# Backward pass of a conditioned spectral and gated block on one core: three loads in the tail are issued at other places

## The chip, the cores and the metric

The kernel runs on one core of a Trainium2 chip. The core has TensorE (PE, matrix products; its weight loads are listed as PEld), VectorE (DVE), ScalarE (ACT), GpSimd (POOL) and SyncE (SP). Each engine works through its own instruction queue in order; semaphores order work between them. DMA transfers are issued here by SP and by POOL and are carried by the core's 16 DMA engines. The metric is the device time of one execution in microseconds (us); a lower time is better. A kernel is timed in several runs, and the median is given.

## The reference

The reference returns the output of a block and the gradients of all its inputs but one. The forward pass, with x of 2048 rows by 576 columns in bfloat16, is

```python
mod = (silu(c) @ w_mod)                 # six rows of 576: sa, ca, ga, sb, cb, gb
h = layernorm(x) * (1 + ca) + sa
x = x + ga * irfft2(rfft2(h) * (w_r + 1j * w_i))      # spectral filter
h = layernorm(x) * (1 + cb) + sb
x = x + gb * (((h @ w_gate) * (h @ w_up)) @ w_down)   # 4608 hidden columns
```

and the kernel computes this output (out_0), the gradients of A_x (out_1), of w_r and w_i (out_2, out_3), w_gate, w_up and w_down (out_4 to out_6), c (out_7) and w_mod (out_8), for a given gradient of the output.

## The kernel before

The 2048 rows lie in 16 tiles of 128 rows, the hidden columns in 36 blocks of 128. The program has three large parts. The first (from line 217) makes the modulation rows, the spectral filter forward, and the gradient of the hidden product (ghhT). The second, which fills most of the time, walks over the 36 hidden blocks: gate and up products (line 647), the gradient with respect to the normalised rows, accumulated by DVE (lines 676 and 681), and the three weight gradients (u57p, line 594). The third part, the tail (from line 731), is where the change lies. It has four stages that overlap:

- the *norm stage* (t1_norm, t1_turn, t1_cols, t1_rows): for each row tile, the backward of the second layernorm, then the forward transforms of the gradient into the buffer Vp. Every second tile, SP loads n2c, goc and yc (two row tiles each, two buffers; line 857). The products n2c with ghr (csA, line 791) and yc with gxr (csC) are column sums for the modulation gradients. The last six weight-gradient products (u57p of the last two hidden blocks) are dealt out between the tiles as filling for PE, and their results are turned and stored by SP (woT, lines 605 to 607).
- the *filter stage* (t2_turn to t2_grad): 19 groups of up to 16 frequencies. Per group four transpositions (trv), products with BD2 (xp), the multiplication with the filter by DVE (fm, line 198, reads wn), transpositions back (try_) and products with BDA (apt). Every fourth group also makes its filter gradient (filter_grad), which loads Xn by POOL and writes its result over wn.
- the *inverse stage* (t3_rows, t3_cols, t3_norm): per row tile the inverse transforms with the tables GB (upa, upb) and IR (yp), and the backward of the first layernorm, with loads n1c and gxc and the store of out_1.
- the *down projection* (u3p, line 1127): out_0 needs for each of 16 row tiles and two halves 36 matmuls of hl (loaded back from hhT_d, nine hidden blocks at a time) with w_down, which lies in wdA (15 blocks) and wdB (21 blocks). These 1152 matmuls depend on none of the three stages; they fill PE's gaps in them and then run alone. The filter gradients that are left (rest) and the modulation sections run beside them.

What sets the order: the kernel is written in a tile framework whose scheduler lays down one fixed order per engine when the program is built, from data dependencies, priorities and a model of costs. The norm stage has raised priority (line 921). `tc.issue_after(ins)` puts what it holds behind `ins` on the engine of `ins`; it adds no wait for the transfer's end. `load_table(pool, key, tag, engine)` loads a constant table into a named slot: RD and IR share slot tA, G1 and GB share tB. Each DMA queue has eight semaphore slots, so an issue waits for the transfer eight places ahead of it.

The places that the change touches: the tile zero (line 757), which is the operand that opens and closes column-sum banks; wn's load from its copy in memory, wn_d, by POOL (line 939); the loads of GB and IR by POOL (lines 1011 and 1012); and wdA's load, in two parts, behind the yc load of tiles 4 and 5 (lines 1100 to 1105).

Of the kernel before, what the change touches and what calls it, by code (L numbers as in the profile page):

```python
# [10 lines left out]
BF = mybir.dt.bfloat16  # L11
# [8 lines left out]
NT = 16  # L20
# [4 lines left out]
FP = 292  # L25
# [59 lines left out]
def build(ctx, tc, A_x, A_w_r, A_w_i, B_w_gate, B_w_up, B_w_down, c_in, w_mod, grad_out,  # L85
          out_0, out_1, out_2, out_3, out_4, out_5, out_6, out_7, out_8):
    nc = tc.nc
# [130 lines left out]
    with ExitStack() as hs:  # L218
        def pool(name, bufs, side="left", space=None, stack=hs):
            kw = dict(name=name, bufs=bufs, reuse_waits="tile")  # L220
            if space is not None:
                kw["space"] = space
            else:
                kw["side"] = side
            return stack.enter_context(tc.tile_pool(**kw))
# [505 lines left out]
    with ExitStack() as ts:  # L731
# [9 lines left out]
        ps_cs = pool("ps_cs", 1, space=PSUM)  # L741
        ps_u3 = pool("ps_u3", 2, space=PSUM)
        tl0 = pool("tl0", 1)
        o2p = pool("o2p", 2)
        oAp = pool("oAp", 1)
        oBp = pool("oBp", 1)
        tl = pool("tl", 1)
        Vp = pool("vp", 1).tile([128, NG, 128], BF, name="b_Vp")
        tl3 = pool("tl3", 1)

        def modh(j, name, pool, eng=nc.sync):
            m = pool.tile([128, D], BF, name=name)
# [1 line left out]
            return m  # L754

        T = {}
        zero = tl3.tile([128, 512], BF, name="zero")
        nc.gpsimd.memset(zero[:], 0.0)
        Vv = Vp[:].rearrange("k g (t c f) -> k g t c f", t=NT, c=2)
        gb_h = modh(MGB, "gb_h", tl, nc.gpsimd)  # L760
# [79 lines left out]
        with ExitStack() as r1:  # L840
            c1 = pool("c1", 2, "right", stack=r1)
            c1b = pool("c1b", 1, "right", stack=r1)
            csA = ps_cs.tile([128, 512], FP32, name="csA")
            csB = ps_cs.tile([128, 512], FP32, name="csB")
            csC = ps_cs.tile([128, 512], FP32, name="csC")
            rings = {k: c1b.tile([128, 3, DP], BF, name=k) for k in ("gyr", "ghr", "gxr")}
            with tc.high_priority(HEAD_START):
                for k in rings:
                    nc.vector.memset(rings[k][:, :, D:DP], 0.0)
            ld, gyTs, zts = {"order": []}, {}, {}  # L850

            def t1_norm(t):
                if t % 2 == 0:
                    for k, src in (("n2c", n2_d), ("goc", go_v), ("yc", y_d)):
                        ld[k] = c1.tile([128, 2, D], BF, name=k)
                        with behind(ld["order"]):
                            ins = nc.sync.dma_start(ld[k][:], src[:, t:t + 2, :])
                        if t == 4:
                            ld["after"] = ins.ins
                    if t < 4:  # L860
                        ld["order"] = [ins.ins]
                        with behind(ld["order"]):
                            for k, tag in ((("RD", "tA"),), (("G1", "tB"), ("BD2", None), ("BDA", None)))[t // 2]:
                                T[k] = load_table(tl0, k, tag)
                        ld["order"] = [tab_ins[k]]
                    ld[t // 2] = (ld["n2c"], ld["yc"])
                n2 = ld["n2c"][:, t % 2, :]
                gh, gx, gy = (rings[k][:, t % 3, 0:D] for k in ("ghr", "gxr", "gyr"))
                nc.scalar.copy(gh, acc(t))
                s12 = c1.tile([128, 2], FP32, name="s12")  # L870
                gn = c1.tile([128, D], BF, name="gn2")
                nc.vector.scalar_tensor_tensor(out=gn[:], in0=acc(t), scalar=1.0, in1=opcb_h[:], op0=MUL, op1=MUL, accum_out=s12[:, 0:1])
                jk = c1.tile([128, D], BF, name="jk2", bufs=1)
                nc.vector.scalar_tensor_tensor(out=jk[:], in0=gn[:], scalar=1.0, in1=n2, op0=MUL, op1=MUL, accum_out=s12[:, 1:2])
                ab = c1.tile([128, 2], FP32, name="ab2")
                nc.vector.tensor_scalar(out=ab[:], in0=s12[:], scalar1=-1.0 / D, scalar2=rstd2g[:, t:t + 1], op0=MUL, op1=MUL)
                u = c1.tile([128, D], BF, name="u2")
                nc.scalar.activation(out=u[:], in_=gn[:], func=ACT.Identity, bias=ab[:, 0:1], scale=rstd2g[:, t:t + 1])
                v = c1.tile([128, D], BF, name="v2", bufs=1)
                nc.vector.scalar_tensor_tensor(out=v[:], in0=n2, scalar=ab[:, 1:2], in1=u[:], op0=MUL, op1=ADD)  # L880
                nc.vector.tensor_tensor(out=gx, in0=v[:], in1=ld["goc"][:, t % 2, :], op=ADD)
                nc.gpsimd.dma_start(gx1_d[:, t, :], gx)
                nc.vector.tensor_tensor(out=gy, in0=gx, in1=ga_h[:], op=MUL)

            def t1_turn(t):
                pt = ps_fp.tile([128, 5, 128], BF, name="trp", tag="fp")
                for m in range(5):
                    nc.tensor.transpose(pt[:, m, :], rings["gyr"][:, t % 3, wide(m)], ident[:])
                gyTs[t] = c1.tile([128, 5, 128], BF, name="gyT")
                nc.scalar.copy(gyTs[t][:], pt[:])  # L890
                gh, gx = rings["ghr"][:, t % 3, :], rings["gxr"][:, t % 3, :]
                n2c, yc = ld[t // 2]
                if t == 0:
                    add_zero(csA, csB, csC, first=True)
                for h in range(2):
                    colsum(csB, h, gh[:, h * 288:(h + 1) * 288])
                diag(csA, csB, 288, gh, n2c[:, t % 2, :])
                diag(csC, csB, 352, gx, yc[:, t % 2, :])
                if t == NT - 1:
                    add_zero(csA, csB, csC, first=False)  # L900

            def t1_cols(t):
                zt = zts[t] = c1.tile([128, 2, FP], BF, name="zt")
                for cc in range(2):
                    zp = ps_fp.tile([128, 512], FP32, name="zp", tag="fp")
                    for m in range(5):
                        with behind(fill[t - 1:t] if t else []):
                            nc.tensor.matmul(zp[:, :FP], lhsT=gyTs[t][:, m, :], rhs=T["RD"][:, m, cc, :], start=(m == 0), stop=(m == 4))  # L908
                    nc.scalar.copy(zt[:, cc, :], zp[:, :FP])

            def t1_rows(t):
                zt = zts[t]
                for cc in range(2):
                    vp = ps_fp.tile([128, 512], FP32, name="vp", tag="fp")
                    nc.tensor.matmul(vp[:, :FP], lhsT=T["G1"][:, t, 0, :], rhs=zt[:, cc, :], start=True, stop=False)
                    nc.tensor.matmul(vp[:, :FP], lhsT=T["G1"][:, t, 2 if cc == 0 else 1, :], rhs=zt[:, 1 - cc, :], start=False, stop=True)
                    evac(Vv[:, :, t, cc, :], vp[:, :FP].rearrange("k (g f) -> k g f", f=4), eng=("a" if cc == 0 else "v"))

            steps = [t1_norm, t1_turn, t1_cols, t1_rows]
            for k in range(NT + len(steps) - 1):  # L920
                with tc.high_priority(HEAD_START + SPREAD * k):
                    for s_ in reversed(range(len(steps))):
                        if 0 <= k - s_ < NT:
                            steps[s_](k - s_)
            after = ld["after"]
            dcb = diag_rows(tl, csA, csB, 288, "dcb")
            dga = diag_rows(tl, csC, csB, 352, "dga")
            dsb = tl.tile([128, 288], FP32, name="dsb")
            nc.vector.tensor_copy(dsb[:], csB[:, 0:288])
# [6 lines left out]
        rA = ts  # L936
        ra = pool("ra", 1, "right", stack=rA)
        wn = ra.tile([128, 2, NT, FP], BF, name="wn2")
        nc.gpsimd.dma_start(wn[:].rearrange("k c a f -> k (c a f)"), wn_d)
        fg = pool("fg", 2, "right", stack=rA)  # L940
        rB = ExitStack()
        A_ = planes(pool("rb", 1, "right", stack=rB), "j_A")
        gYs = {}

        def dims(ci):
            ng = min(4, NG - 4 * ci)
# [2 lines left out]
        def filter_grad(ci):  # L949
            g0, ng, f0, w = dims(ci)  # L950
            Xn = fg.tile([128, 2, NT, 16], BF, name="Xn2")
            nc.gpsimd.dma_start(Xn[:].rearrange("k c a f -> k (c a f)"), xn_d[:, ci * 512:(ci + 1) * 512])
            t1 = fg.tile([128, 2, 2, NT, 16], FP32, name="gwt", bufs=1)
            for i in range(2):
                if w == 16:
# [7 lines left out]
        with ExitStack() as r2:  # L963
# [44 lines left out]
                    filter_grad(ci)  # L1008

            pipeline(NCH, [t2_turn, t2_filter, t2_back, t2_inv, t2_grad])  # L1010
        T["GB"] = load_table(tl0, "GB", "tB", nc.gpsimd)
        T["IR"] = load_table(tl0, "IR", "tA", nc.gpsimd)
        r3 = ExitStack()
        c3 = pool("c3", 2, "right", stack=r3)
        c3b = pool("c3b", 1, "right", stack=r3)
# [81 lines left out]
        wdA = oAp.tile([128, 15, D], BF, name="wdA")  # L1097
        wdB = oBp.tile([128, NFB - 15, D], BF, name="wdB")

        def wd_load(dst, k, f0, n):  # L1100
            with tc.issue_after(after):
                nc.sync.dma_start(dst[:, k:k + n, :], B_w_down[f0 * 128:(f0 + n) * 128, :].rearrange("(j f) d -> f j d", f=128))

        wd_load(wdA, 0, 0, 8)
        wd_load(wdA, 8, 8, 7)
        prs = {}
        for tp_ in range(NT // 2):
            hls = []
# [118 lines left out]
```

## Time and profile before

| | |
|---|---|
| runs | 1585.85, 1587.19, 1590.39 us; median 1587.19 |
| profiled execution: span from first to last instruction (its own time is listed in no other form) | 1583.9 us, 29938 instructions |
| PE busy | 1526.4 us, 96% |
| DVE busy | 1043.3 us, 66% |
| ACT busy | 559.4 us, 35% |
| POOL busy | 172.3 us, 11% |
| mean granted clock of TensorE | 0.990 |
| DMA | 280.33 MB, 177 GB/s on average |
| tail, 1230 to 1584 us: PE busy | 316.6 us |

The page gives busy time and idle time by engine, the waits by what ended them, the chain of work that ended last, and the DMA issues with their time from issue to landing. A busy PE is not a PE at its peak, because matmuls are pipelined and their ends are modelled: a u3p matmul of 288 columns is listed with 0.286 us, but 72 of them follow each other in 8.82 us. Idle time of an engine that is not the bound costs nothing. Positions are microseconds from the start of the span.

### The profile page before, as it was taken

The numbers are of one execution on the slowest core, as the hardware profiler recorded it, in microseconds if no ns is written. First come the engines' busy times: TensorE is split into PE (matmuls) and PEld (weight loads), VectorE is DVE, ScalarE is ACT, GpSimd is POOL, SyncE is SP. The second block draws the span as 40 slices with busy tenths as digits, with TensorE's granted clock in tenths as the row PEclk, the third lists the DMA queues.
The fourth block names the chain that finished last, engine by engine and source line by source line (L and its number), as shares of the span: only waits on it lengthen the run. The fifth ranks groups of instructions, "written<-read, shape, count | busy, mean of one in ns | idle before, by whom it ended". The sixth has DMA issues, their size and how long they took to land.

```text
span 1583.9 us, 29938 instructions
## 1 busy us (share of the span) xinstructions
PE 1526.4 (96%) x11300; PEld 1028.1 (65%) x11306; DVE 1043.3 (66%) x2626; ACT 559.4 (35%) x1120; POOL 172.3 (11%) x285
## 2 busy tenths in 40 slices
PE   6999999999999999999999999999999979799997
PEld 4665543566666666667666666766666666577775
DVE  6866663766666666666666666666666765678655
ACT  6667732322222222222222222222222356465022
POOL 0001221110010101001010100101000002000232
PEclk9999999999999999999999999999999999999999
DMA  9879997868685795877767786858976777547775
GB/s 323 268 197 235 289 261 211 172 133 158 123 177 114 159 153 118 168 132 155 141 148 136 143 163 122 173 116 144 139 141 137 193 207 200 212 144 214 278 228 156
DMA packets 485252, 280.33 MB, mean 177 GB/s; under 512 B 407634, under 2 KB 452435, under 8 KB 484211
## 3 DMA queue, kind: packets, MB, share of 16 engines
q1 hardware_dynamic: 459922, 185.50, 54.9%
q0 software_dynamic: 25184, 92.92, 19.7%
q8 instruction: 88, 1.44, 0.4%
q14 instruction: 58, 0.47, 0.1%
HBM read 108.48 MB, written 82.31 MB: 120 GB/s over the span
## 4 chain that ended last, share of the span: by engine, by line
PE 81%; DVE 6%; DMA 5%; issue 4%; ACT 3%; POOL 0%; SPq 0%; ACTq 0%; DVEq 0%; POOLq 0%
PE u57p L594 26%; PE u8p L676 18%; PE gup L647 16%; PE u4p L408 7%; PE u3p L1127 4%; PE gup L642 2%; DMA Xn<-xn_d 2%; DMA n2c<-n_d 2%; PE yp L186 1%; PE zp L908 1%; ACT u L1055 1%; PE zp L346 1%; DVE ln_st L151 1%; DMA xc<-in_A_x_dram 1%; DMA hh_sf<-hhT 1%
## 5 line engine op out<-in xcount | busy, mean ns | idle before, releaser
L681 DVE TENSOR_TENSOR acc<-acc,u8p 128x288 f32<-128x288 f32 x1088 | 489.2, 454 | 314.6 <-PE u8p L676 314.2
L676 PE MATMUL u8p<-wT,ggT 128*128 128x288 bf16 x1152 | 327.5, 286 | 1.7 <-DVE acc L681 1.7
L676 PE MATMUL u8p<-wT,guT 128*128 128x288 bf16 x1152 | 327.2, 286 | 0.0
L647 PE MATMUL gup<-h2T,wgu 128*128 128x512 bf16 x1152 | 294.9, 379 | 0.0
L597 ACT CAST so<-u57p 128x288 bf16<-128x288 f32 x216 | 86.0, 398 | 521.4 <-PE u57p L594 515.5
L594 PE MATMUL u57p<-gon,hh_sf 128*128 128x288 bf16 x1152 | 188.5, 286 | 0.5 <-DMA hh_sf<-hhT 0.5
L594 PE MATMUL u57p<-h2p,gg_sf 128*128 128x288 bf16 x1152 | 187.9, 286 | 0.0
L594 PE MATMUL u57p<-h2p,gu_sf 128*128 128x288 bf16 x1152 | 185.9, 286 | 0.0
L647 PEld LDWEIGHTS <-wgu 128*128 128x128 bf16 x1152 | 109.5, 98 | 98.8 <-issue 17.1
L676 PEld LDWEIGHTS <-ggT 128*128 128x128 bf16 x1152 | 112.6, 98 | 67.2 <-issue 14.0
L408 PE MATMUL u4p<-goT,wdT 128*128 128x512 bf16 x656 | 151.6, 380 | 0.6 <-DVE goT L380 0.5
L676 PEld LDWEIGHTS <-guT 128*128 128x128 bf16 x1152 | 112.7, 98 | 55.8 <-issue 2.2
L1127 PEld LDWEIGHTS <-hl 128*128 128x128 bf16 x1152 | 111.9, 99 | 32.9 <-issue 5.9
L594 PEld LDWEIGHTS <-hh_sf 128*128 128x128 bf16 x1152 | 112.7, 98 | 29.2 <-DMA hh_sf<-hhT 0.8
L594 PEld LDWEIGHTS <-gu_sf 128*128 128x128 bf16 x1152 | 112.5, 98 | 28.4
L594 PEld LDWEIGHTS <-gg_sf 128*128 128x128 bf16 x1152 | 112.5, 98 | 28.2
L649 ACT CAST gT<-gup 128x512 bf16<-128x512 f32 x144 | 84.3, 586 | 130.7 <-PE gup L647 130.7
L649 ACT CAST uT<-gup 128x512 bf16<-128x512 f32 x144 | 84.3, 585 | 73.5 <-PE gup L647 73.5
L408 PEld LDWEIGHTS <-wdT 128*128 128x128 bf16 x656 | 61.4, 98 | 73.1 <-issue 8.0
L1127 PE MATMUL u3p<-wdB,hl 128*128 128x288 bf16 x672 | 94.8, 290 | 5.3 <-DMA wdB<-in_B_w_down_dram 5.3
L660 POOL DMA_DIRECT2D hhT_d<-hhT x36 | 33.2, 921 | 504.4 <-DVE hhT L651 475.5
L141 ACT CAST ghh_st<-u4p 128x512 bf16<-128x512 f32 x88 | 51.2, 585 | 65.2 <-PE u4p L408 63.7
(357 smaller groups left out, 1701.7 us busy)
## 6 DMA issues: line engine op xcount, KB each, us to landing
ghhT_d<-ghh_st POOLq DMA_DIRECT2D x36, 512.0 KB, 4.4
ghh<-ghhT_d POOLq DMA_DIRECT2D x36, 512.0 KB, 7.3
hhT_d<-hhT POOLq DMA_DIRECT2D x36, 512.0 KB, 6.6
hl<-hhT_d SPq DMA_DIRECT2D x32, 576.0 KB, 7.2
out_dram<-woT SPq DMA_DIRECT2D x72, 128.0 KB, 2.0
wdn<-in_B_w_down_dram SPq DMA_DIRECT2D x18, 288.0 KB, 3.9
out_dram<-so SPq DMA_DIRECT2D x36, 144.0 KB, 2.6
wgu<-in_B_w_gate_dram SPq DMA_DIRECT2D x18, 256.0 KB, 3.4
```

What stands on the lines that cost most here:

```text
L141: nc.scalar.copy(dst, src)
L151: nc.vector.bn_stats(out=st[:, t, h, :], in_=xt[:, t, h * 288:(h + 1) * 288])
L408: nc.tensor.matmul(pt[:], lhsT=wdTs[k][:, j, m, :], rhs=goT[:, 4 * sb4:4 * sb4 + 4, m, :], start=(m == 0 and n == 5), stop=(m == n - 1))
L594: mm = nc.tensor.matmul(pw[0][:, 0:288], lhsT=sf[:, t, :], rhs=rhs_n[:, t, h * 288:(h + 1) * 288], start=(t == 0), stop=(t == NT - 1))
L597: nc.scalar.copy(so[:, h * 288:(h + 1) * 288], pw[0][:, 0:288])
L642: nc.tensor.matmul(pts[-1][:], lhsT=wgu[r, 8, jw * 128:(jw + 1) * 128], rhs=h2T[r, 4 * sb4:4 * sb4 + 4, 4, :], start=True, stop=False)
L647: nc.tensor.matmul(pts[k][:], lhsT=wgu[:, 4 * wi_ + m, jw * 128:(jw + 1) * 128], rhs=h2T[:, ts_, m, :], start=False, stop=(m == 3))
L649: nc.scalar.copy((gT, uT)[wi_][:, ts_, :], pts[k][:])
L660: nc.gpsimd.dma_start(hhT_d[:, :, fb, :].rearrange("tp f x -> f tp x"), hhT[:].rearrange("f (tp ti) p -> f tp (ti p)", ti=2))
L676: nc.tensor.matmul(pu[:, 0:288], lhsT=l_, rhs=r_, start=(k == 0), stop=(k == len(mms) - 1))
L681: nc.vector.tensor_tensor(out=dst, in0=dst, in1=pu[:, 0:288], op=ADD)
L1127: mm = nc.tensor.matmul(p2[:, 0:288], lhsT=hls[fb // 9][:, fb % 9, ti * 128:(ti + 1) * 128], rhs=(wdA[:, fb] if fb < 15 else wdB[:, fb - 1 ...
```

## The change

Four places of the tail are edited.

- The filter copy wn is loaded by SP instead of POOL, in two halves, behind the last of the norm stage's loads (`ld["final"]`, yc of tiles 14 and 15).
- wdA is loaded in three parts of five blocks instead of two parts of eight and seven; the parts are put behind the yc loads of tiles 6, 8 and 10 (`ld["y", t]`) instead of 4.
- The loads of GB and IR, still on POOL, are put behind the Xn loads of the groups 4 and 8.
- The tile zero moves from a pool of its own at the end into the pool of the tables, so that what lies between them in memory moves up by its 1 KB per partition.

```diff
         tl0 = pool("tl0", 1)
+        zero = tl0.tile([128, 512], BF, name="zero")
         o2p = pool("o2p", 2)
...
-        tl3 = pool("tl3", 1)
...
-        zero = tl3.tile([128, 512], BF, name="zero")
         nc.gpsimd.memset(zero[:], 0.0)
...
                             ins = nc.sync.dma_start(ld[k][:], src[:, t:t + 2, :])
                         if t == 4:
                             ld["after"] = ins.ins
+                        ld["final"] = ld["y", t] = ins.ins
...
-        nc.gpsimd.dma_start(wn[:].rearrange("k c a f -> k (c a f)"), wn_d)
+        for c in range(2):
+            with tc.issue_after(ld["final"]):
+                nc.sync.dma_start(wn[:, c].rearrange("k a f -> k (a f)"), wn_d[:, c * NT * FP:(c + 1) * NT * FP])
...
-        gYs = {}
+        gYs, xn_in = {}, {}
...
-            nc.gpsimd.dma_start(Xn[:].rearrange("k c a f -> k (c a f)"), xn_d[:, ci * 512:(ci + 1) * 512])
+            xn_in[ci] = nc.gpsimd.dma_start(Xn[:].rearrange("k c a f -> k (c a f)"), xn_d[:, ci * 512:(ci + 1) * 512]).ins
...
-        T["GB"] = load_table(tl0, "GB", "tB", nc.gpsimd)
-        T["IR"] = load_table(tl0, "IR", "tA", nc.gpsimd)
+        for k, tag, ci in (("GB", "tB", 4), ("IR", "tA", 8)):
+            with tc.issue_after(xn_in[ci]):
+                T[k] = load_table(tl0, k, tag, nc.gpsimd)
...
-        def wd_load(dst, k, f0, n):
-            with tc.issue_after(after):
+        def wd_load(dst, k, f0, n, behind_=None):
+            with tc.issue_after(behind_ or after):
                 nc.sync.dma_start(dst[:, k:k + n, :], B_w_down[f0 * 128:(f0 + n) * 128, :].rearrange("(j f) d -> f j d", f=128))
 
-        wd_load(wdA, 0, 0, 8)
-        wd_load(wdA, 8, 8, 7)
+        for k in range(0, 15, 5):
+            wd_load(wdA, k, k, 5, ld["y", 6 + 2 * (k // 5)])
```

## The prediction

> **What bounds the kernel now.** I read the page's busy shares first, then the stretches of the last 345 us cut at the places where TensorE (PE) has no work, then PE's waits, and last the DMA issues behind those waits.
>
> ```profile
> PE 1526.4 (96%) x11300; PEld 1028.1 (65%) x11306; DVE 1043.3 (66%) x2626; ACT 559.4 (35%) x1120; POOL 172.3 (11%) x285
> ```
>
> PE is the bound of the whole, so what can be won is time in which PE stands still or runs at a lower clock. Time by stretch in the tail (columns: stretch, its length, busy us of each engine, granted clock, DMA share, GB/s):
>
> ```profile
> 1288.80:1295.50 6.70, 0.01 (x1) 0.01 (x1) 1.32 (x3) 1.03 (x3) 0.13 (x1) 0.88 1.18 333
> 1295.50:1301.50 6.00, 6.00 (x40) 4.57 (x40) 3.63 (x10) 1.90 (x4) 1.08 (x2) 0.56 0.31 74
> 1301.50:1342.80 41.30, 37.95 (x340) 27.94 (x340) 21.65 (x53) 26.06 (x55) 6.77 (x14) 1.00 0.67 182
> 1350.90:1356.40 5.50, 0.18 (x3) 0.10 (x2) 1.25 (x4) 0.95 (x2) 0.00 (x0) 0.90 1.01 376
> 1356.40:1362.10 5.70, 5.70 (x33) 4.24 (x33) 1.68 (x5) 1.66 (x3) 0.00 (x0) 0.50 1.08 379
> 1362.10:1404.40 42.30, 38.74 (x412) 28.35 (x411) 34.46 (x104) 25.43 (x54) 4.39 (x8) 1.00 0.41 139
> 1404.40:1457.00 52.60, 50.08 (x448) 37.86 (x449) 42.71 (x110) 35.74 (x84) 0.55 (x1) 1.00 0.56 161
> 1457.00:1571.00 114.00, 113.29 (x903) 89.67 (x902) 71.18 (x182) 23.29 (x45) 31.93 (x54) 1.00 0.75 241
> ```
>
> Two holes, each with the DMA engines full and each followed by some 6 us at about half the clock. What ended them, and the transfers around them (waits: us in total, times, longest; issues: KB, us to landing; SP and POOL by time; chain: start, us):
>
> ```profile
> PE csA L791 <- DMA n2c<-n_d: 8.1, 4, 6.7
> PE u3p L1127 <- DMA wdB<-in_B_w_down_dram: 5.3, 1, 5.3
> ...
> wn<-wn_d POOLq DMA_DIRECT2D x1, 2336.0 KB, 12.3
> wdB<-in_B_w_down_dram SPq DMA_DIRECT2D x1, 1584.0 KB, 19.6
> wdA<-in_B_w_down_dram SPq DMA_DIRECT2D x1, 1008.0 KB, 7.0
> ...
> 1282.06 0.54 POOL L939 DMA_DIRECT2D wn<-wn_d  x1
> 1285.95 9.50 DMA n2c<-n_d
> 1328.56 0.59 SPq L1102 DMA_DIRECT2D wdA<-in_B_w_down_dram  x1
> 1339.92 0.43 SPq L1102 DMA_DIRECT2D wdB<-in_B_w_down_dram  x1
> ```
>
> The filter copy (wn) starts at 1282.06, and the n2c load of tiles 10 and 11, issued 3.9 us later, takes 9.5 us; the median of the eight n2c loads is 3.2. The second hole is wdB, which queues behind 2160 KB of wdA.
>
> **The change, part by part.** The page gives the profiled execution only its span, 1583.9 us. The three timed runs lie 2.0 to 6.5 us above that, their median 3.3; I sum on the span and add 3.3. One u3p matmul costs 0.1225 us (72 in 8.82 us on the chain).
>
> (a) *Filter copy out of the norm stage's loads.* It goes from POOL to SP behind the last yc load, as two halves. The hole is worth at most 6.7 us plus the low clock after it, 6.0 x (1 - 0.56) = 2.6. But the norm chain runs on VectorE (DVE): between 1282 and 1320 DVE idles 5.9 us for n2c and 2.5 us for an ACT u behind it, so 8.4 is the upper end. In its place come three wdA pieces of 720 KB on SP, behind the yc loads of tiles 6, 8 and 10. By 7.0 us for 1008 KB a piece lands in about 5.0 us (estimate); the second is issued some 2 us ahead of the n2c that was late, and may hold it up to 3 us. Ahead of that n2c's first matmul the built order now has 33 u57 matmuls where it had 6, which is 3.3 us more cover. (That n2c's issue also waits for the first piece to land, eight issues back on SP; the piece has 11 us for it.) I take 6.5: all of the direct 5.9 and a little of the 2.5. The lower end is a loss, rival C.
>
> [...]
>
> (b) *wdA early, seen from PE.* The built order puts 12 u3p matmuls ahead of the filter stage's first transposition: 1.5 us, against 1.9 us of PE waits there for ACT and DVE between 1333 and 1343 (five of 0.25 to 0.65). Cost 0 to 1.5, taken 0.5. The first needs hl, which SP now issues right behind the last u57 matmul (1331.4 on the old clock) and PE reaches it at 1335.9; hl lands in 3.7 us at best and 7.2 in the median, so it costs 0 to 2.7; with few transfers ahead of it I take 0.5. Behind that hl's wait stand, in SP's queue, the last woT transpose, the second hl and wdB; the first two are not late by it, since the transpose needs the same product, and wdB is counted in (c).
>
> (c) *The second hole* is worth 5.5 + 5.7 x 0.50 = 8.4. wdB's first part is issued behind the last woT store, at about 1336.5 instead of 1339.9, and needs not wait for wdA. From there to the fourth hl go 4.4 MB, 11.9 us at the 373 GB/s of 1340 to 1365; with 2.1 us before the first byte (3.7 for an hl, less its 1.6 of data) that ends at 1350.5. PE reaches the matmuls that need it at about 1349. The table GB (1.57 MB, POOL) still falls into this stretch, since its queue neighbour, the second Xn load, was already ahead of it: the order asked for moves IR behind the third Xn (1341.4 to 1348) but GB not at all. GB can add up to 4.2 us. Wait left 0 to 5.6, taken 3.0; gain 5.4.
>
> (d) *Filter stage.* From its first transposition to the inverse stage's first matmul PE has 246 u3p matmuls instead of 223: 2.8 us, against 3.6 us of PE idle between 1362.1 and 1404.4. Cost 0 to 2.8, taken 1.4.
>
> (e) *Inverse stage.* 33 u3p matmuls instead of 61, worth 3.4 us if PE set its pace. DVE's instructions there sum to 50.3 us of 53, so it does not; gain 0 to 3.4, taken 0.5.
>
> (f) *What is left after it*: 861 u3p matmuls instead of 868, 0.9 us, in a stretch where PE has no gap.
>
> At nothing I cost: the issues (SP: five large DMAs of 0.6 us, in a queue that waits for DVE and PE before nearly every load of the norm stage; if that cover went, 0.6 each); wn's later landing (1310.6 + 12.3 = 1323, first read by fm at 1344.9; 22 us cover); IR (landing 1356, first read 1405.7); the zero tile's move, which puts a 0.5 us memset ahead of POOL's last hhT store, with its wait on an earlier gate/up matmul; and the n1c loads of the inverse stage, now behind two hl loads that wait for PE, still about 5.7 us ahead of their use with a 3.3 us landing.
>
> Sum: 6.5 - 0.5 - 0.5 + 5.4 - 1.4 + 0.5 + 0.9 = 10.9. Span 1573.0, time 1576.3 us.
>
> **The rivals.**
> B: the second hole stays as it is. GB and the hl loads share the engines with wdB, the wait is 5 us or more and the low clock comes with it. For it: the DMA share is 1.02 from 1340 to 1365 and only wdA's part of that leaves; against it: wdB starts 3.4 us earlier. Without 5.4 the time is 1581.7. [...]
>
> C, slower: the wdA pieces hold up the activations. A row shows that it can happen: the n2c load issued at 1241.13, right behind the 730 KB table RD on SP, took 9.14 us, 5.9 over the median. Three such holes are 17.7 us, and if the clock falls behind each, 7.9 more, in place of 9.3 cured: with (b) to (f) as summed the time is about 1599. It decides for slower (by 0.3%) from waits of 3.5 us each with the clock falling, 6.2 without. Against it: the DMA share is 0.49 from 1262 to 1282, where it was above 1 when that load was late.
>
> D, nothing: the bytes only change places and DMA engines bound the tail anyway, so each wait comes back elsewhere. Against it: the engines are at 0.51 from 1296 to 1328, 16 us of free time, and the 2.4 MB of wn need 6.4 at 373 GB/s. Only (f) remains, 1586.3.
>
> **How the numbers follow.** No change and a change are told apart here by about 0.3%, 4.8 us, so faster is below 1582.4. The forecast 0.68, B 0.15, D 0.07, C 0.10. B lies on the border and is split, 0.08 faster and 0.07 same. Faster 0.76, same 0.14, slower 0.10. The ends of the terms give 1566 (8.4 + 8.4 + 3.4 + 0.9 won) at one side and beyond 1590 at the other. The range that leaves out no more than 2 in 10 runs from 1568, where (a) and (c) are nearly whole, to 1585, which takes in B with a part of D.
>
> **What would show it.** Right: no PE wait on n2c above 2 us and full clock from 1280 to 1330; norm stage's end some 6 us earlier; a PE wait on wdB or hl of 0 to 5 us; u3p matmuls between the last vp matmuls; an inverse stage of 51 to 53 us. Wrong: n2c landing 6 us or more after its issue with wdA in front of it (C); PE waiting 5 us or more in the filter stage, or the first u3p matmul holding up the norm stage's last column matmuls (B); the filter stage as much longer as the norm stage is shorter (DVE in (d) sets its pace).

## The result and the profile after

The changed kernel takes 1581.51 us (median of 20 runs, 1573.54 to 1588.41), the kernel before 1588.41 us beside it (20 runs, 1582.80 to 1595.09). The ratio is 0.9949, with a 95% interval of 0.9931 to 0.9966: it is faster by 6.9 us, where 10.9 were forecast. The forecast of 1576.3 us lay 5.2 us too low; 1581.5 lies in the stated range, and within 0.2 us of what rival B would have given. (Counted as a gain, B's 5.5 us stand against 6.9 measured: the forecasts start from 1587.19 us, the median of three runs, and the kernel before is at 1588.41 over twenty.)

The profiled execution of the changed kernel lies above its own median (1584.98 us, span 1583.2). Its span is therefore no measure of the change; it has to be cut at a mark. PE starts the last 128 u8p matmuls here, right behind its last gate and up products, and the 8608 matmuls up to this mark are the same number in every kernel of this document (timeline of PE, first line before, second line after; columns: start, us, engine, line, operation):

```profile
1236.35 0.29 PE L676 MATMUL u8p<-wT,ggT 128*128 128x288 bf16 x1
```
```profile
1242.36 0.29 PE L676 MATMUL u8p<-wT,ggT 128*128 128x288 bf16 x1
```

The execution of the changed kernel reached this mark 6.0 us later. The busy shares of the whole (page) have hardly moved:

```profile
PE 1528.7 (97%) x11306; PEld 1028.2 (65%) x11306; DVE 1041.3 (66%) x2626; ACT 560.0 (35%) x1120; POOL 172.3 (11%) x284
```

So the reading goes by stretches. From the mark to the last product (gcp), before against after:

| stretch, from PE's timeline | before us | after us | won us | forecast |
|---|---|---|---|---|
| mark to first csA | 24.8 | 24.4 | 0.4 | 0 |
| norm stage, first csA to first trv | 81.6 | 77.8 | 3.8 | (a), (b): 5.5 |
| filter stage, to first upa | 61.6 | 62.2 | -0.6 | (c), (d): 4.0 |
| inverse stage, to the last yp | 48.2 | 46.8 | 1.4 | (e): 0.5 |
| what is left, to the last gcp | 127.2 | 125.5 | 1.7 | (f): 0.9 |
| sum, called the tail below | 343.4 | 336.8 | 6.6 | 10.9 |

The tail of this one profile gained 6.6 us, about what the medians gained. Time by stretch after the change (columns as before the change: stretch, length, busy us of PE, PEld, DVE, ACT and POOL, granted clock, DMA share, GB/s):

```profile
1285.00:1318.20 33.20, 29.71 (x289) 21.96 (x287) 29.73 (x78) 22.22 (x43) 6.47 (x12) 1.00 1.01 296
1318.20:1320.20 2.00, 0.00 (x0) 0.00 (x1) 0.46 (x1) 0.00 (x0) 0.00 (x0) 0.95 0.28 113
1320.20:1323.60 3.40, 3.40 (x20) 2.20 (x21) 0.00 (x0) 0.79 (x2) 1.61 (x3) 0.53 0.50 144
...
1345.40:1348.20 2.80, 0.09 (x2) 0.00 (x1) 0.00 (x0) 0.21 (x1) 0.00 (x0) 0.84 1.04 377
1348.20:1355.00 6.80, 6.80 (x45) 4.96 (x45) 3.13 (x9) 1.59 (x4) 1.06 (x2) 0.56 1.04 394
...
1358.20:1360.40 2.20, 0.06 (x1) 0.00 (x0) 0.94 (x4) 0.63 (x2) 0.00 (x0) 1.00 1.02 418
1360.40:1363.90 3.50, 3.47 (x26) 2.92 (x26) 1.68 (x5) 1.66 (x3) 0.00 (x0) 0.58 0.48 193
1363.90:1406.70 42.80, 42.10 (x433) 30.48 (x431) 34.57 (x105) 25.44 (x55) 4.93 (x9) 0.99 0.35 115
1406.70:1455.00 48.30, 43.92 (x400) 33.67 (x400) 39.29 (x104) 35.14 (x82) 1.61 (x3) 1.00 0.62 184
1455.00:1569.00 114.00, 114.00 (x913) 90.45 (x912) 72.62 (x183) 24.27 (x46) 30.74 (x51) 1.00 0.74 237
```

The large hole of the norm stage is gone: from 1285 to 1318 PE runs at full clock, with the DMA engines full (1.01). Where there was one hole in each stage there are now three shorter ones, 2.0, 2.8 and 2.2 us, and each has a stretch at about half the clock behind it. (A stretch whose edges do not fall on those of the slow clock shows a mean between 0.5 and 1.) What ended them, from the waits of PE and of DVE (us in total, times, longest), the DMA issues (KB, us from issue to landing) and the chain (start, us):

```profile
PE u3p L1130 <- DMA wdB<-in_B_w_down_dram: 4.9, 2, 2.7
PE csA L790 <- DMA n2c<-n_d: 2.9, 4, 1.4
PE csC L790 <- DVE gxr L881: 2.4, 2, 2.1
...
DVE gxr L881 <- DMA gx_d<-gxr: 2.4, 1, 2.4
...
wn<-wn_d SPq DMA_DIRECT2D x2, 1168.0 KB, 10.5
wdB<-in_B_w_down_dram SPq DMA_DIRECT2D x1, 1584.0 KB, 19.0
T_GB<-tab_GB POOLq DMA_DIRECT2D x1, 1536.0 KB, 10.1
wdB<-in_B_w_down_dram SPq DMA_DIRECT2D x1, 1440.0 KB, 8.9
...
1291.03 6.05 DMA n2c<-n_d
1310.96 8.64 DMA gx_d<-gxr
1341.39 19.00 DMA wdB<-in_B_w_down_dram
```

The n2c waits fell from 8.1 to 2.9 us. The wait at csC is new: DVE can't write gxr for the last tile, because the gx_d store issued at 1310.96 takes 8.6 us beside wn, which SP had issued at 1308.55. In the filter stage the two parts of wdB are now each waited for. The first (1440 KB) lands in 8.9 us; before, PE's wait for it ended 16.5 us after its issue. The second (1584 KB) takes 19.0 us, and took 19.6 before, when PE came too late to wait for it. wdA has left the queue ahead of wdB, but the time that the second part takes from issue to landing has hardly changed. Counted from the first trv it lands 3.7 us earlier (at 15.8 us against 19.5), mostly because it is issued 3.1 us earlier.

### The profile page after: what moved, and what is told of

Same layout as the page of the kernel before. It is cut to its first block, busy times and chain, and to the rows that moved or that the text cites. A ratio compares the mean times of both kernels' runs of the same rounds, so it can differ in the third digit from the quotient of the medians.

```text
span 1583.2 us, 29948 instructions
## 1 busy us (share of the span) xinstructions
PE 1528.7 (97%) x11306; PEld 1028.2 (65%) x11306; DVE 1041.3 (66%) x2626; ACT 560.0 (35%) x1120; POOL 172.3 (11%) x284
## 3 DMA queue, kind: packets, MB, share of 16 engines
q1 hardware_dynamic: 460226, 187.89, 55.4%
## 4 chain that ended last, share of the span: by engine, by line
PE 85%; DMA 7%; DVE 5%; ACT 2%; issue 1%; SPq 0%; POOL 0%; DVEq 0%; ACTq 0%
PE u57p L594 26%; PE u8p L676 18%; PE gup L647 16%; PE u3p L1130 8%; PE u4p L408 7%; PE gup L642 2%; DMA xc<-in_A_x_dram 2%; DMA n2c<-n_d 2%; DMA wdB<-in_B_w_down_dram 1%; DMA n1c<-n_d 1%; PE yp L186 1%; PE zp L908 1%; PE zp L346 1%; DVE ln_st L151 1%; PE u4p L403 1%
## 5 line engine op out<-in xcount | busy, mean ns | idle before, releaser
L676 PEld LDWEIGHTS <-guT 128*128 128x128 bf16 x1152 | 112.7, 98 | 55.4 <-issue 1.9
L408 PEld LDWEIGHTS <-wdT 128*128 128x128 bf16 x656 | 61.4, 98 | 77.2 <-issue 12.4
L143 DVE CAST ghh_st<-u4p 128x512 bf16<-128x512 f32 x56 | 38.7, 690 | 54.5 <-PE u4p L408 54.4
```

Source lines behind the costliest of these rows:

```text
L143: nc.vector.tensor_copy(dst, src)
L408: nc.tensor.matmul(pt[:], lhsT=wdTs[k][:, j, m, :], rhs=goT[:, 4 * sb4:4 * sb4 + 4, m, :], start=(m == 0 and n == 5), stop=(m == n - 1))
L676: nc.tensor.matmul(pu[:, 0:288], lhsT=l_, rhs=r_, start=(k == 0), stop=(k == len(mms) - 1))
```

## The experiments

Lengths of stages are from one profile of each kernel, cut at the mark as above. Two profiles of one and the same program (e3 and e11 below) differ by 1.8 us in the tail, so a smaller difference between two single profiles says nothing. Ratios are to the kernel before, run in the same group, with 95% intervals.

| run | norm | filter | inverse | left | tail us | ratio |
|---|---|---|---|---|---|---|
| changed kernel | 77.8 | 62.2 | 46.8 | 125.5 | 336.8 | 0.9949 (0.9931 to 0.9966) |
| e1 wn alone | 80.4 | 61.3 | 48.2 | 127.9 | 342.3 | 0.9969 (0.9945 to 0.9993) |
| e2 wdA alone, zero not moved | 81.0 | 60.4 | 47.2 | 128.3 | 341.3 | 0.9989 (0.9967 to 1.0011) |
| e12 wdA alone, zero moved, tables in the new order | 80.8 | 60.5 | 46.4 | 125.7 | 338.1 | 0.9985 (0.9964 to 1.0007) |
| e7 before, tables later | 80.4 | 54.2 | 48.2 | 127.0 | 334.3 | 0.9961 (0.9941 to 0.9981) |
| e10 before, wn and tables later | 75.4 | 55.4 | 48.2 | 127.7 | 331.0 | 0.9930 (0.9902 to 0.9957) |
| e3 changed, tables later | 75.5 | 55.9 | 45.0 | 125.5 | 326.2 | 0.9898 (0.9869 to 0.9928) |
| e11 the same again | 77.5 | 55.7 | 45.2 | 125.5 | 328.0 | 0.9883 (0.9860 to 0.9906) |
| e9 changed, GB alone later | 77.2 | 57.4 | 45.4 | 125.5 | 329.9 | 0.9896 (0.9862 to 0.9929) |
| e4 changed, wn behind the stores | 76.9 | 62.0 | 46.0 | 125.5 | 334.7 | 0.9936 (0.9912 to 0.9960) |
| e5 e3 and e4 together | 77.3 | 54.4 | 45.1 | 125.5 | 326.8 | 0.9935 (0.9907 to 0.9963) |
| e6 e3, wdB ahead of hl | 77.4 | 57.1 | 48.2 | 125.6 | 332.7 | 0.9933 (0.9908 to 0.9958) |
| e8 changed, waits filled | 75.7 | 61.2 | 49.0 | 127.2 | 337.7 | 0.9966 (0.9948 to 0.9984) |

### The parts alone

e1 makes the kernel before load wn as the changed kernel does, and nothing else:

```diff
+                        ld["final"] = ld["y", t] = ins.ins
...
-        nc.gpsimd.dma_start(wn[:].rearrange("k c a f -> k (c a f)"), wn_d)
+        for c in range(2):
+            with tc.issue_after(ld["final"]):
+                nc.sync.dma_start(wn[:, c].rearrange("k a f -> k (a f)"), wn_d[:, c * NT * FP:(c + 1) * NT * FP])
```

> The kernel before with one part of the change alone: the filter copy wn goes in two halves to SP, behind the last of the norm stage's loads; w_down and the tables stay as before. Theory (each moved transfer meets other work at its new place, and a PE wait costs its length and half of the slow-clock stretch behind it): the n2c hole of 6.7 us and its slow clock go; in their place DVE waits some 2 us for a gx_d store behind wn at about 1318 us, with or without a fall of the clock; norm stage, first csA to first trv, 81.6 us before, to 76 to 79; filter stage unchanged within 2 us, its wait on wdB stays at 5 to 6 us; time 3 to 5 us below before, ratio 0.997 to 0.998. Rival (the bytes only change places, nothing won): ratio 0.999 to 1.001. Rival (the hole came from another transfer than wn): the n2c wait stays above 5 us.

Its waits, of PE and of DVE:

```profile
PE u3p L1130 <- DMA wdB<-in_B_w_down_dram: 5.3, 1, 5.3
PE csC L791 <- DVE gxr L882: 3.5, 3, 3.0
PE csA L791 <- DMA n2c<-n_d: 3.4, 3, 2.3
...
DVE gxr L882 <- DMA gx_d<-gxr: 3.1, 1, 3.1
```

As the theory had it: wn was what held n2c, the wait on gx_d comes with wn's new place and with nothing else, and the wait on wdB stays as it was. The time fell by about 5 us; the one profile shows only 1.2 us in the norm stage, short of the 3 to 6 expected, since two of its waits (2.3 and 3.0 us) each had a slow stretch behind them. That profiled execution, 1589.94 us, was one of the slowest of the twelve.

e2 leaves wn alone and edits only wdA's load, in three pieces behind the yc loads of tiles 6, 8 and 10:

```diff
+                        ld["final"] = ld["y", t] = ins.ins
...
-        def wd_load(dst, k, f0, n):
-            with tc.issue_after(after):
+        def wd_load(dst, k, f0, n, behind_=None):
+            with tc.issue_after(behind_ or after):
...
-        wd_load(wdA, 0, 0, 8)
-        wd_load(wdA, 8, 8, 7)
+        for k in range(0, 15, 5):
+            wd_load(wdA, k, k, 5, ld["y", 6 + 2 * (k // 5)])
```

> The kernel before with the other part alone: wdA in three pieces behind the yc loads of tiles 6, 8 and 10; wn stays with POOL at its old place. Theory: the n2c hole stays, and is longer by up to 3 us for the wdA piece that SP issues ahead of that n2c (6 to 9 us in all); in the filter stage the wait on wdB stays at 4 to 6 us in one or two parts, since GB and the hl loads still share the engines with it; what is won is at most the 1 to 2 us of the u3p matmuls done earlier; ratio 0.998 to 1.003. Rival (the whole gain of the change comes from wdA, by freeing the stretch in which wdB loads): ratio 0.994 to 0.996.

The ratio came out as expected, but the run tests less than it was meant to. SP's timeline has the pieces where wdA always was:

```profile
1327.97 0.59 SPq L1103 DMA_DIRECT2D wdA<-in_B_w_down_dram  x1
1333.01 0.59 SPq L1103 DMA_DIRECT2D wdA<-in_B_w_down_dram  x1
1335.79 0.58 SPq L1103 DMA_DIRECT2D wdA<-in_B_w_down_dram  x1
```

In the changed kernel the first is issued at 1280.58. `issue_after` names the earliest place only. e12 is the same part with the tile zero moved as well and GB and IR in their new order, that is the changed kernel with wn put back:

```diff
-        for c in range(2):
-            with tc.issue_after(ld["final"]):
-                nc.sync.dma_start(wn[:, c].rearrange("k a f -> k (a f)"), wn_d[:, c * NT * FP:(c + 1) * NT * FP])
+        nc.gpsimd.dma_start(wn[:].rearrange("k c a f -> k (c a f)"), wn_d)
```

> The changed kernel with wn alone put back to POOL at its old place. It differs from the run of wdA alone above by the move of the tile zero: there the three pieces of wdA were issued at 1328 to 1336 us all the same, here the built order has them behind the yc loads of tiles 6, 8 and 10. Theory (wdA early only moves the late part of the stage): the n2c hole is back and longer, 6.7 to 10 us, since a wdA piece and wn share the engines with that n2c; in the filter stage waits on wdB as in the changed kernel, 4 to 6 us in all, because GB still fills the engines beside it; u3p matmuls left after the inverse stage as in the changed kernel (125.5 us); tail 340 to 346 us against 336.8 in the changed kernel and 343.4 before; ratio to before 0.997 to 1.002. Rival (wdA early is what the change gains by): tail 335 to 339 us, ratio 0.994 to 0.996.

Here the pieces were issued at 1285.65, 1293.76 and 1304.14. So one of the two further edits lets wdA go early, and no run parts them. The move of zero, priced in the prediction as a memset in POOL's queue, is the likely one, since it shifts wdA's place in memory, which may then become free earlier; this was not tested. The stalls are as the theory expected: PE waits 7.6 us for n2c, which takes 12.3 us to land with wn and a wdA piece beside it, and 5.6 us for wdB in two waits. The tail of its profile, 338.1 us, is the rival's; the ratio (0.9964 to 1.0007) leaves out the rival's 0.996 only just, and can't be told from no change. So wn alone gives some 5 us, the rest of the change some 2 (-1 to 6), and both together 6.9.

### What makes wdB late

The prediction named the 2160 KB of wdA in front of wdB. e7 leaves them there, and wn where it was, and only moves the two tables behind the fourth Xn load; e3 and e11 do that in the changed kernel; e9 moves GB alone:

```diff
 e7, kernel before (xn_in as in the changed kernel)
...
-        T["GB"] = load_table(tl0, "GB", "tB", nc.gpsimd)
-        T["IR"] = load_table(tl0, "IR", "tA", nc.gpsimd)
+        for k, tag, ci in (("GB", "tB", 12), ("IR", "tA", 12)):
+            with tc.issue_after(xn_in[ci]):
+                T[k] = load_table(tl0, k, tag, nc.gpsimd)
 e3 and e11, changed kernel
-        for k, tag, ci in (("GB", "tB", 4), ("IR", "tA", 8)):
+        for k, tag, ci in (("GB", "tB", 12), ("IR", "tA", 12)):
 e9, changed kernel
-        for k, tag, ci in (("GB", "tB", 4), ("IR", "tA", 8)):
+        for k, tag, ci in (("IR", "tA", 8), ("GB", "tB", 12)):
```

> The kernel before with one edit: GB and IR behind the fourth Xn load; wn and wdA as before. Theory (the tables' 2.3 MB, 6 us of full engines, make wdB late in the kernel before too): the 5.3 us wait on wdB falls to 0 to 2 and its slow clock goes; filter stage 61.6 us to 54 to 58; the n2c hole stays at 6 to 7 us; ratio 0.994 to 0.996. Rival (wdA's 2.2 MB in front of wdB in the same queue make it late, as the prediction had it): the wait stays at 4 us or more, filter stage 60 us or more, ratio 0.998 to 1.001.

> The changed kernel with GB and IR both behind the fourth Xn load (some 1369 us instead of 1344 and 1353). Theory (2.3 MB of tables share the engines with wdB and make it late): the second wait on wdB (2.2 us) and its slow clock of 3.4 us go, the first (2.7 us) shortens by up to 1; filter stage, first trv to first upa, 62.2 us in the changed kernel, to 57 to 60; inverse stage unchanged; ratio to before 0.991 to 0.994. Rival (the hl loads and wdB fill the engines by themselves, 5.5 MB in one queue): both waits stay within 1 us, ratio 0.994 to 0.996. Rival (DVE sets the filter stage's pace): the waits go and the stage still takes 61 us or more.

> The changed kernel with GB alone behind the fourth Xn load; IR stays behind the third (some 1353 us). Theory (GB, 1.57 MB issued at 1344.3, is what fills the engines beside wdB; IR comes when wdB's last part is nearly in): the waits on wdB as with both tables moved, 1.5 to 3 us in all instead of 4.9; filter stage 62.2 us to 55.5 to 58; ratio to before 0.989 to 0.993. Rival (IR's 0.74 MB at 1353 makes the second wait): a second wait of 1 us or more at 1358 to 1361 us with slow clock stays, filter stage 59 to 62 us, ratio 0.992 to 0.995.

PE's waits between 1260 and 1375 us in e7 (the longest two; there is none on wdB or hl) and its DMA issues:

```profile
PE csA L791 <- DMA n2c<-n_d: 7.4, 3, 6.1
PE try__16777 L995 <- DVE Ygc L989: 1.5, 1, 1.5
...
wdB<-in_B_w_down_dram SPq DMA_DIRECT2D x1, 1584.0 KB, 14.3
T_GB<-tab_GB POOLq DMA_DIRECT2D x1, 1536.0 KB, 6.9
```

With all of wdA still ahead of it in SP's queue, wdB's second part lands in 14.3 us instead of 19.6, the wait on wdB is gone and the filter stage is 7.4 us shorter. The n2c hole stays, since wn stays. The same in the changed kernel, e9 and then e11:

```profile
PE u3p L1130 <- DMA wdB<-in_B_w_down_dram: 2.2, 1, 2.2
...
wdB<-in_B_w_down_dram SPq DMA_DIRECT2D x1, 1584.0 KB, 12.6
T_GB<-tab_GB POOLq DMA_DIRECT2D x1, 1536.0 KB, 6.7
```
```profile
PE u3p L1130 <- DMA wdB<-in_B_w_down_dram: 1.6, 1, 1.6
...
wdB<-in_B_w_down_dram SPq DMA_DIRECT2D x1, 1584.0 KB, 12.1
T_GB<-tab_GB POOLq DMA_DIRECT2D x1, 1536.0 KB, 6.6
```

GB alone takes 6.4 us off wdB's second part (19.0 to 12.6), IR another 0.5. The second wait is gone in both. So it is GB on POOL's queue, issued at 1344.26 beside wdB, that sets the filter stage. GB itself lands in 6.7 us instead of 10.1, long before the inverse stage reads it. The first part of wdB hung on the tables too: in e7, with wdA still in front, the hl load issued right behind that part landed in 11.1 us instead of 17.3. Counted from the first trv, wdB's second part lands at 19.5 us in the kernel before, at 15.8 in the changed kernel, at 13.7 in e7 and at 8.9 in e11. So wdA's place moves that landing by 4 to 5 us, and the tables' place by 6 to 7.

e11 put e3's kernel beside e9 and e10 on one chip:

> The changed kernel with GB and IR behind the fourth Xn load, once more, beside the two other kernels of this group on one chip. Both theories: tail within 2 us of 326.2, no slow clock between 1300 and 1500 us or one stretch of 3.4; ratio to before within 0.987 to 0.993. If the 0.9898 of its first six runs was a low draw, as the runs of the kernel with both edits (0.9935) suggest: 0.991 to 0.994.

It gave 1572.30 us against 1590.45 before, ratio 0.9883. It beats e10 (1579.48 us; the intervals of the two ratios touch only at their ends), while from e9 (1574.10 us) it can't be told. By the intervals of the table it is faster than the changed kernel, as e3 is.

e10 takes wn late and the tables late, and leaves wdA where it was:

> The kernel before with wn late on SP and both tables behind the fourth Xn load; wdA stays behind the norm stage. Theory (once the tables are out of the way, wdA's early place is worth only the u3p matmuls that fill waits, 2 to 4 us): filter stage 54 to 56 us, norm stage 77 to 80.5, what follows the inverse stage 127 to 128 us against 125.5; tail 328 to 331 us against 326.2 with wdA early too; ratio to before 0.992 to 0.994. Rival (wdA early is needed for wdB to be in time, and the tables alone sufficed only because the n2c hole delayed PE): a wait on wdB of 3 us or more returns, filter stage 58 us or more, ratio 0.995 or above.

There is no wait on wdB at all, and the filter stage takes 55.4 us, as in e3 and e11. What is lost against them (1579.48 against 1572.30 us in one group) lies behind it: 3.0 us in the inverse stage and 2.1 in what is left, since fewer u3p matmuls were done early: 28 more fall into the inverse stage, 3.4 us at 0.1225 us each, and 7 more behind it (0.9 us of the 2.1). This is what wdA's early place, with the move of zero, is worth once PE doesn't stand waiting for wdB.

### Other places for wn and wdB

e4 is the changed kernel with wn's halves put on POOL behind the last gx_d store:

```diff
-            with tc.issue_after(ld["final"]):
-                nc.sync.dma_start(wn[:, c].rearrange("k a f -> k (a f)"), wn_d[:, c * NT * FP:(c + 1) * NT * FP])
+            with tc.issue_after(ld["stored"]):
+                nc.gpsimd.dma_start(wn[:, c].rearrange("k a f -> k (a f)"), wn_d[:, c * NT * FP:(c + 1) * NT * FP])
```

(`ld["stored"]` is the instruction of the last gx_d store.)

> The changed kernel with wn's two halves on POOL, behind the norm stage's last gx_d store (some 1321 us) instead of on SP at 1308.6. Theory (wn fills the engines while the gx_d stores of the last tiles run, and DVE's gxr waits for its buffer): DVE's 2.4 us wait for gx_d goes, and with it PE's 2.05 us wait at csC and the slow clock of 3.4 us behind it; norm stage, 77.8 us in the changed kernel, to 74 to 75; wn lands by about 1335, before its first use; filter stage unchanged within 1 us; ratio to before 0.992 to 0.994. Rival (the last tile's chain through DVE, PE and ACT sets the end of the norm stage anyway, wait or not): ratio 0.994 to 0.996 with a norm stage of 77 us or more.

Waits of PE, and one of SP:

```profile
PE u3p L1130 <- DMA wdB<-in_B_w_down_dram: 7.4, 2, 4.6
...
PE u3p L1130 <- DMA hl<-hhT_d: 2.1, 1, 2.1
...
SPq L606 <- DMA woT<-so: 9.7, 2, 7.2
```

The wait on gx_d is gone, but PE waits 2.1 us for the first hl. That hl takes 4.1 us to land, no more than elsewhere, and wn has landed before it is issued; what is late is its issue. The woT transposition ahead of it in SP's queue, issued at 1313.76 with wn in flight (1310.50 to 1320.18), lands in 8.6 us instead of 3.3, and SP waits 7.2 us for it before it can store the result and issue hl. PE, now without the wait at csC, comes to its first u3p matmul 2.9 us earlier after the mark, while hl is issued only 0.8 us earlier. A wait of 1.9 us on n2c had a slow stretch behind it besides, so the norm stage is 0.9 us shorter instead of 3. What PE then gains it spends waiting for wdB. The ratio can't be told from that of the changed kernel.

e5 joins this with the tables of e3:

> The changed kernel with both edits: GB and IR behind the fourth Xn load, and wn on POOL behind the last gx_d store. Theory (waits are cured one by one where the transfer in front is moved): no wait on gx_d, at most one short wait on wdB, no slow clock between 1300 and 1500 us; tail from the last block's first u8p to the last instruction 326.2 us with the tables alone moved, to 323 to 327; ratio to before 0.987 to 0.990. Rival (wn at 1321 to 1335 now lies in front of hl and wdB, as with wn moved alone, where the waits on wdB grew to 7.4 us and a wait of 2.1 on hl was new): waits on wdB and hl of 3 us or more with slow clock, ratio 0.991 to 0.994, worse than the tables alone.

The wait on wdB is down to 0.3 us, but the wait on hl (2.3 us, with one slow stretch) stays; woT's transposition again takes 9.0 us beside wn. The tail of its profile is as good as that of e3 and e11, yet its median was 1579.06 us and its ratio 0.9935. The profiled execution, 1568.24 us, was the fastest of its nine, so the profile does not show what held up the others. Why it is no better, or even worse, than the tables alone stays open.

e6 takes e3 and issues wdB ahead of the hl loads:

```diff
-                if tp_ == 0 and b0 in (9, 18):
-                    wd_load(wdB, 10 * (b0 // 9 - 1), 15 + 10 * (b0 // 9 - 1), 9 + b0 // 9)
...
+        for k, n in ((0, 10), (10, 11)):
+            wd_load(wdB, k, 15 + k, n, ld["final"])
         prs = {}
```

> The changed kernel with the tables later as before and wdB issued ahead of the hl loads (behind the last product of the second part, some 1332 us, instead of 1339 and 1341); the built order then has no u3p matmul before the first transposition of the filter stage. Theory (the queue's order decides who waits): no wait on wdB; hl comes 5 to 8 us later than now, and PE has other work of the filter stage until then or waits up to 3 us for hl; norm stage 1.5 us shorter by the 12 matmuls that leave it; ratio 0.987 to 0.991. Rival (hl takes wdB's place as the late one, 5 us or more, with slow clock): ratio 0.992 to 0.995.

Neither wdB nor hl is waited for. The norm stage is not shorter, though, and the inverse stage is back at 48.2 us, because the built order then has fewer u3p matmuls ahead of it (232 before the inverse stage, 258 in e3). PE also waits 1.9 us for DVE at csD, with a slow stretch behind it. A miss on both sides: the wait was cured, the order was worse.

### Filling the waits

e8 puts matmuls that add zero into the first u3p bank, 22 ahead of the first block that reads wdB and 18 ahead of the first that reads its second part:

```diff
                     for fb in range(NFB):
+                        for _ in range({15: 22, 25: 18}.get(fb, 0) if t == h == 0 else 0):
+                            nc.tensor.matmul(p2[:, 0:288], lhsT=ident[:], rhs=zero[:, 0:288], start=False, stop=False)
```

> The changed kernel with 40 more matmuls that add zero to the first u3p bank (22 ahead of the first block that reads wdB, 18 ahead of the first that reads its second part; 0.1225 us each, 4.9 us in all), where PE now waits 2.7 and 2.2 us. Theory (the clock falls by half for one or two stretches of 3.4 us when PE has stood still for more than some 1.9 us of one such stretch): with the waits filled no stretch is idle for so long, the 10.2 us of slow clock between 1347 and 1365 us shrink to 3.4 or none, and the filter stage, 62.2 us, comes to 57 to 61 although 4.9 us of matmuls were added; ratio 0.992 to 0.995. Rival (the clock falls for another reason, or the slow stretches cost nothing because DMA or DVE set the pace): slow clock of 6.8 us or more, filter stage 62 to 67 us, ratio 0.995 to 0.998.

Time by stretch around them:

```profile
1347.50:1353.00 5.50, 5.25 (x55) 3.80 (x53) 4.97 (x14) 2.20 (x5) 1.87 (x4) 1.00 1.03 409
1353.00:1358.00 5.00, 3.60 (x37) 2.58 (x37) 2.93 (x9) 2.92 (x6) 0.00 (x0) 1.00 1.04 380
1358.00:1362.00 4.00, 0.43 (x2) 0.10 (x1) 0.00 (x0) 0.00 (x0) 0.00 (x0) 0.86 1.05 405
1362.00:1368.00 6.00, 5.94 (x36) 4.45 (x37) 2.79 (x7) 2.06 (x4) 0.61 (x1) 0.52 0.14 56
```

The first wait was filled, and no slow stretch followed it: so far the theory holds. But PE then stood 4.0 us at the second part of wdB, with 6.8 us of slow clock behind it. That part landed 15.3 us after the stage's first transposition, and in the changed kernel 15.8. The first wait and its slow stretch had cost almost nothing of their own: the landing of the second part is what PE has to meet. The filter stage is 1.0 us shorter with 4.9 us of added matmuls, and the time (0.9966) is not better than that of the changed kernel; as a repair, the filling failed.

## Why the prediction was right in sign and too high

*(a), 6.5 forecast, some 5 found.* The hole went, and with it its slow clock. Waits on n2c fell by 5.2 us and 6.8 us of half clock (3.4 us) went; against this stand the new wait on gx_d (2.05 us and half of a slow stretch of 3.4, 3.75 in all) and 12 u3p matmuls that are now in the norm stage (1.5 us). That gives 3.4 us; the stage gained 3.8. The term missed that wn would slow POOL's stores of the last tiles. wn's landing was priced at nothing because fm reads it late; who shares the engines with it at its new place was not asked. The wdA pieces landed in 6.7 to 7.4 us, not in the estimated 5.0. The n2c issued at 1291.03, 1.3 us behind the second wdA piece, landed in 6.05 us, where the median of the eight before was 3.2; in the seven other kernels that have the two in this order (e3 to e6, e8, e9, e11) it took between 4.1 and 6.6 us. The wait cost PE 1.4 us, with the 33 u57 matmuls in front of it.

*(b), -1.0 forecast.* The 12 matmuls are there; hl was not waited for.

*(c), +5.4 forecast, -1.3 found.* This is the step that failed. It took a residual wait of 3.0 us (from 0 to 5.6) and no slow clock. Waits fell only from 5.3 to 4.9 us, and the slow clock grew from 6.8 to 10.2 us: (5.3 + 3.4) - (4.9 + 5.1) = -1.3. The transfers, up to the fourth hl, were forecast to end at 1350.5, with GB adding up to 4.2 us. On the old clock (6.0 us less) wdB's second part landed at 1354.4 and that hl at 1355.8, although the first part was issued at 1333.3 and not at 1336.5. GB is the term that was too small: by e9 it costs wdB's second part 6.4 us. And PE, forecast to come to the matmuls in question at 1349, came to its first wdB matmul at 1339.5 on that clock, 0.9 us after the first trv where the kernel before came to it after 8.3, and to the second part at 1352.3. The cause given, wdA ahead of wdB, was only a part: it held up wdB's first part (16.5 to 8.9 us, in which the tables had a share), but the stage waits for the second, and e7 and e9 show that this hangs most on GB. The row quoted for it, 19.6 us, belonged to wdB's second part, so that the reading took the one for the other.

*(d), -1.4 forecast, +0.7 found.* Without waits and slow clock the filter stage was 52.9 us before (61.6 - 5.3 - 3.4) and 52.2 after (62.2 - 4.9 - 5.1), with 23 u3p matmuls more: they fitted into its gaps.

*(e) and (f), 0.5 and 0.9 forecast, 1.4 and 1.7 found.* The right sign, both a little small. e3, e9 and e11 have 125.5 us left as well, and e7, without wdA early, 127.0. The reason for taking only 0.5 in (e), that DVE sets the pace there, does not hold: the stage takes 48.2 us in each of the four kernels with 61 u3p matmuls in it (before, e1, e7, e10), and 45.0 to 45.4 with 33 of them in e3, e5, e9 and e11, nearly the whole 3.4 us of the difference. The changed kernel stayed at 46.8 because PE waited 3.4 us in all for n1c, a load that the prediction had put at nothing; before there was no such wait, and in e3 it is 1.4 us.

*The rivals.* B is what happened, in its own mechanism: GB and the hl loads share the engines with wdB (DMA share 1.04 from 1345.4 to 1355.0), some 5 us of waiting stay and the slow clock comes with it. It had been given 0.15. That its price, 1581.7 us, was met so closely is partly luck: (c) came out 6.7 us below the forecast and (a) and (b) 1.7, and (d), (e), (f) and the start of the tail gave 4.2 back. C did not happen, though the sign named for it did show (an n2c that landed in 6.05 us behind a wdA piece): no PE wait on n2c is above 1.4 us. Of the signs for a right forecast, the n2c waits came true, but the norm stage ended 4.2 us earlier and not 6, and the clock fell at 1319.98. D is refuted by e3, e9 and e11, which move the same bytes and stand at 0.9883 to 0.9898.

## What to carry to other kernels

When a load is moved, list what every other queue has in flight between its issue and its landing, and ask of each when it is needed: GB was needed 60 us later and ran beside the load that PE stood waiting for. Moving the transfer with the latest need gave more in the filter stage (54.2 us in e7) than moving what stood ahead of the late transfer in its own queue (60.5 in e12). Price a PE wait with the slow clock behind it (in the changed kernel 3.41, 6.83 and 3.41 us at half clock behind waits of 2.05, 2.7 and 2.17 us), and compare two profiles from a mark ahead of the edit, since the spans of one program differ by more than such a change is worth (1571.8 to 1586.6 us over the twenty runs of the changed kernel).

## What the runs showed of the hardware that was not expected

*A wait of 2.05 us had 3.41 us at half clock behind it.* Between 1230 and 1455 us of six profiles (the kernel before, the changed kernel, e9 to e12) the slow stretches are 3.41 or 6.83 us long. In the changed kernel they start at 1319.98, 1347.29 and 1360.94, that is 8 and 4 times 3.41 us apart. This kernel, cut from these starts in steps of 3.41 us:

```profile
1296.09:1299.50 3.41, 2.38 (x30) 2.09 (x30) 2.40 (x8) 1.15 (x3) 0.54 (x1) 1.00 1.17 197
1299.50:1302.91 3.41, 3.09 (x29) 2.06 (x28) 3.34 (x9) 3.41 (x7) 0.54 (x1) 1.00 1.08 367
...
1316.57:1319.98 3.41, 1.48 (x12) 0.71 (x9) 1.06 (x3) 0.78 (x2) 0.00 (x0) 1.00 0.65 260
1319.98:1323.40 3.42, 3.20 (x16) 2.00 (x17) 0.17 (x1) 0.59 (x2) 1.61 (x3) 0.50 0.43 120
...
1343.88:1347.29 3.41, 1.57 (x14) 0.96 (x13) 0.46 (x1) 0.86 (x2) 0.53 (x1) 1.00 1.07 385
1347.29:1350.70 3.41, 2.50 (x16) 1.89 (x16) 0.74 (x3) 1.07 (x2) 0.00 (x0) 0.50 1.07 417
...
1357.53:1360.94 3.41, 1.24 (x12) 0.83 (x12) 1.26 (x4) 1.30 (x3) 0.00 (x0) 1.00 1.01 411
1360.94:1364.36 3.42, 3.42 (x26) 2.80 (x24) 1.68 (x5) 1.66 (x3) 0.00 (x0) 0.50 0.33 131
```

and two steps of e4, neither followed by slow clock:

```profile
1326.32:1329.73 3.41, 1.81 (x15) 1.44 (x16) 0.46 (x1) 0.91 (x3) 0.44 (x1) 1.00 1.02 311
1336.56:1339.97 3.41, 1.57 (x18) 1.35 (x18) 0.25 (x1) 0.86 (x2) 0.00 (x0) 1.00 1.04 401
```

In the changed kernel a step at full clock in which PE is idle for 1.93, 1.84 or 2.17 us (length less PE's busy time) is followed by one at half; with 1.03 us idle it is not. Between 1230 and 1455 us of the six profiles, each cut in such steps, half clock followed the eight steps at full clock with 1.97 to 3.41 us idle and none of those with 1.73 us or less. Between these lie 1.93 and 1.84 us in the changed kernel, where it followed, and 1.84 us in the kernel before, where it did not; nor did it follow the 1.84 us of e4 above. From half clock it went back to full behind steps with 0 to 0.24 us idle, and stayed at half behind 0.91 (changed kernel), 1.06 and 1.60 (before) and 2.95 us (e12). So the length of a wait alone did not give its price: the changed kernel waited 2.05 us at csC, with 1.93 us idle in one step, and a slow stretch followed, while e4 waited 2.06 us for hl, with 1.60 us idle in one step, and none did.

*Transfers took longer beside one of the other queue.* GB took 10.1 us beside wdB and 6.7 without it (e9); wdB's second part 19.0 with GB and 12.6 without. A woT transposition on SP took 8.6 and 9.0 us beside wn on POOL (e4, e5) and 3.3 in the changed kernel, where wn had landed.

*One program, two arrivals.* The profiles of e3 and e11, the same kernel, reach the mark at 1244.18 and 1233.88 us. These 10.3 us lie ahead of the tail, and all of them in the program's first part: the same matmuls are 0.1 us apart at 113 us, 3.1 at 173, 10.5 at 255, and then 10.3 all through the second part. PE waited 9.1 us for DVE and ACT between 113 and 256 us in the later execution and 1.7 in the other, and only the later one had slow clock there (6.8 us). A difference of this size is most of the spread of the runs of one kernel (14.9 us for the changed one); that it makes that spread, and what holds up DVE and ACT there, was not followed up.
